# Attention backward: the last value and key gradient sums written in bfloat16 over their float32 tiles, with a third buffer of turned gradients

## The chip, the core and the metric

The kernel runs on one core of one Trainium2 chip. The metric is the device time of one execution in microseconds, the median of several executions. A profile of one execution is given as well; its times are those of that execution.

## What is computed

The reference is a gated mix of an attention block and a state-space convolution, with all gradients. Only the attention's gradients matter here. Cut to them:

```python
qkv = (x @ wqkv).reshape(B, S, 3, H, Dh).transpose(2, 0, 3, 1, 4)   # S 2048, H 32, Dh 18
q, k, v = qkv[0], qkv[1], qkv[2]
p = softmax(einsum("bhqd,bhkd->bhqk", q, k) * Dh ** -0.5)
o = einsum("bhqk,bhkd->bhqd", p, v)
out = g * (o @ wo) + (1 - g) * b          # g: a sigmoid gate, b: the convolution
# and the gradients of out, by jax.vjp, for x, wqkv, wo, the convolution's parameters and the gate
```

For a head the kernel needs dV (the sum over queries of p times dO), dQ and dK (sums over keys and over queries of dS = p * (dP - row sum)). They are stored in one array in DRAM, `dqkv_d`, which a later stage multiplies with the weights and with x.

## The kernel before

**Stages.** Projections and preparations come first (to about 205 us in the profile), then the attention with its backward pass in one long interleaved loop (to about 2197 us), then the convolution with its gradients, and the output products (to the end). The change touches the attention loop alone, which is called the attention stage below.

**Units.** The 32 heads are worked in 8 groups of 4 (`g`), the 2048 queries in 4 blocks of 512 (`b`). A unit is one group and one query block; there are 32. A unit takes 32 steps (`G` counts the steps of all units). A unit's forward part (scores with keys on the partitions, line 723, exponentials at line 799) runs OFF = 39 steps ahead of its backward part (scores again, line 766, exponentials at line 804; dP at line 774; `ds` = dP times p, line 809).

**Order.** The order of the instructions on TensorE (PE), ScalarE (ACT), VectorE (DVE), GpSimd (POOL) and the queue of SyncE (SP) is that in which this loop emits them (`manual_schedule`, line 436). Nothing is moved past anything else on the same engine. Each step has one slot of eight for a part of the sums (lines 677 and 728 to 758): value gradient in slots 0 and 1, query gradient in 2 and 3, a turn of `ds` tiles on PE in 4 and 7, key gradient in 5 and 6. So eight steps handle one key block `kq` of 512 keys, and the four of a unit take `kq` 0 to 3. All sums and turns pass through one PSUM buffer (`accB`, line 588): the next one's first matmul waits until DVE has taken the one before.

**The sums.** For a key block, dV and dK are added up over the four query blocks in float32 tiles in SBUF, four for dV (`dvacc`, line 606) and four for dK (`dkacc`, line 643): a copy at b = 0, an add in place at b = 1 and 2 (lines 612 and 649). At b = 3 the add writes to a bfloat16 tile `gb` instead, which comes from `grad_tile` (line 526) and has two buffers for all callers. dQ is complete after the four key blocks of each unit, and its last write goes to a `gb` tile too (line 630). So a unit with b < 3 takes one `gb` tile and a unit with b = 3 takes nine, in the order v0 k0 v1 k1 v2 k2 v3 q k3, where a k comes five steps after its v, the next v three steps after that, q two steps after v3, and k3 three after q. With two buffers, a write takes the buffer of the write before the last: q that of k2, five steps later, k3 that of v3, five steps later, and the others one that was written eight steps before.

**Storing.** Two steps after a sum is complete `store_grad` (line 529) puts a transposing DMA of the `gb` tile on SP's queue (line 532, to one of two `gT` buffers), and four steps later `pack` copies `gT` without its padding to `dtk` on POOL (line 536) and starts the DMA to `dqkv_d` from POOL's queue (line 537). A `gb` buffer is free when its transposing DMA has landed, a `gT` buffer when POOL has read it.

**SP's queue.** It also starts the 512 transposing DMAs of `ds` (line 817), which the key gradient sums read as `dsT` (line 639), and the loads of the next K, Q, V pieces. A waiting DMA on it holds all behind it. `ds` has five buffers, freed by those DMAs, among others.

The lines that decide the order of the tiles (`nm` V, Q or K, `h` the half of a sum):

```python
SLOTS = {0: ("V", dv_half, 0), 1: ("V", dv_half, 1), 2: ("Q", dq_half, 0), 3: ("Q", dq_half, 1), 5: ("K", dk_half, 0), 6: ("K", dk_half, 1)}
...
if nm == "Q" and kq == NQ - 1:
    at(("pre", G + 2), lambda g=g, b=b: store_grad(UN[(g, b)].pop("dqa"), g, 0, b * TPQ))
elif nm in "KV" and b == NQ - 1:
    at(("pre", G + 2), lambda g=g, kq=kq, nm=nm: store_grad(DKV.pop((nm.lower(), g, kq)), g, 1 + "KV".index(nm), kq * TPQ))
```

Of the kernel before, what the change touches and what calls it, by code (L numbers as in the profile page):

```python
# [11 lines left out]
BF = mybir.dt.bfloat16  # L12
# [5 lines left out]
P = 128  # L18


def build(tc, aps, dbg_aps=None, stages=("s1", "attn", "post", "s4", "final")):
# [7 lines left out]
    def mm(out, lhsT, rhs, start=True, stop=True, **kw):  # L29
        return nc.tensor.matmul(out, lhsT=lhsT, rhs=rhs, start=start, stop=stop, **kw)  # L30
# [13 lines left out]
    HP = 32  # L44
# [17 lines left out]
    with ExitStack() as gctx:  # L62
# [53 lines left out]
        with ExitStack() as ctx:  # L116
            s1 = ctx.enter_context(tc.tile_pool(name="s1", bufs=1))
            work = ctx.enter_context(tc.tile_pool(name="s1work", bufs=2))
# [310 lines left out]
        if "attn" in stages:  # L429
            KB = 512  # L430
            NQ = S // KB
            TPQ = KB // P
            DA = HP
            NFILL = {"V": 1, "Q": 0, "K": 0}
            with ExitStack() as ctx:
# [3 lines left out]
                work = ctx.enter_context(tc.tile_pool(name="awork", bufs=2))  # L439
# [41 lines left out]
                DKV = {}  # L481
# [42 lines left out]
                    return f0, f1, f2  # L524

                def grad_tile():
                    return work.tile([P, KB], BF, tag="gb", bufs=2, name="gb")

                def store_grad(gb, g, which, t0):
                    c0 = which * D + g * 4 * DH  # L530
                    gT = work.tile([P, TPQ, 4, HP], BF, tag="gT", bufs=2, name="gT")
                    nc.sync.dma_start_transpose(out=gT.rearrange("p t a b -> p t (a b)"), in_=gb)

                    def pack():
                        dtk = work.tile([P, TPQ, 4, DH], BF, tag="dtk", bufs=1, name="dtk")
                        nc.gpsimd.tensor_copy(dtk, gT[:, :, :, 0:DH])
                        nc.gpsimd.dma_start(dqkv_d[:, t0:t0 + TPQ, c0:c0 + 4 * DH], dtk.rearrange("p t a b -> p t (a b)"))
                    packs.append((now[0] + 4, pack))
# [10 lines left out]
                def by_pe(p):  # L549

                    return {NPF: 0, NPF + 1: 1}.get(p, 2)
# [15 lines left out]
                def ds_tiles(U, p):  # L567

                    n = by_pe(p)
                    return [U["ds"][2 * p + 2 - n + x][:, 3, :] for x in range(n)], [(n, lambda: U["dsT", p][:, 2 - n:2, 3 * TPQ:, :])]  # L570
# [26 lines left out]
                def dv_half(g, b, kq, h, acc):  # L597
                    U = UN[(g, b)]
                    for ii in (2 * h, 2 * h + 1):
                        for j in range(4):  # L600
                            mm(acc[HP * j:HP * (j + 1), :], lhsT=U["dOa"][:, ii, j, :], rhs=U["eb"].pop((kq, ii, j)),
                               start=(ii == 0), stop=(ii == 3), tile_position=(0, HP * j))

                    def ev():
                        if b == 0:
                            DKV[("v", g, kq)] = work.tile([P, KB], F32, tag="dvacc", bufs=4, name="dvacc")
                            nc.vector.tensor_copy(DKV[("v", g, kq)], acc)
                            return
                        a_ = o_ = DKV[("v", g, kq)]
                        if b == NQ - 1:  # L610
                            o_ = DKV[("v", g, kq)] = grad_tile()
                        nc.vector.tensor_tensor(o_, a_, acc, op=A.add)  # L612
                    return ev

                def dq_half(g, b, kq, h, acc):
                    U = UN[(g, b)]
                    for n_ in (2 * h, 2 * h + 1):
                        for j in range(4):
                            mm(acc[HP * j:HP * (j + 1), :], lhsT=grp_t[g]["Ktok", kq][:, n_, HS * j:HS * j + HP], rhs=U["ds"][TPQ * kq + n_][:, j, :],
                               start=(n_ == 0), stop=(n_ == 3), tile_position=(0, HP * j))  # L620

                    def ev():
                        if kq == 0:
                            U["dqa"] = work.tile([P, KB], F32, tag="dqa", bufs=1, name="dqa")
                            nc.vector.tensor_scalar(U["dqa"], acc, c_scale, None, op0=A.mult)
                            return
                        a_ = o_ = U["dqa"]
                        if kq == NQ - 1:
                            o_ = U["dqa"] = grad_tile()
                        nc.vector.scalar_tensor_tensor(o_, acc, c_scale, a_, op0=A.mult, op1=A.add)  # L630
                    return ev

                def dk_half(g, b, kq, h, acc):
                    U = UN[(g, b)]
                    o_ = acc[:, 2 * h * P:2 * (h + 1) * P]
                    for qb in range(TPQ):
                        for j in range(4):
                            mm(o_[HP * j:HP * (j + 1), :].rearrange("p (a b) -> p a b", b=P), lhsT=grp_t[g]["Qtok", b][:, qb, HP * j:HP * (j + 1)],
                               rhs=U["dsT", 2 * kq + h][:, :, j * TPQ + qb, :], start=(qb == 0), stop=(qb == TPQ - 1), tile_position=(0, HP * j))

                    def ev():
                        if b == 0:
                            DKV[("k", g, kq)] = work.tile([P, KB], F32, tag="dkacc", bufs=4, name="dkacc")
                            nc.vector.tensor_copy(DKV[("k", g, kq)], acc)
                            return
                        a_ = o_ = DKV[("k", g, kq)]
                        if b == NQ - 1:
                            o_ = DKV[("k", g, kq)] = grad_tile()
                        nc.vector.tensor_tensor(o_, a_, acc, op=A.add)
                    return ev  # L650

# [50 lines left out]
                for G in range(NTOT + OFF + 24):  # L702
# [4 lines left out]
                    if G < NTOT:  # L707
                        u, s = divmod(G, NST)
                        g, b = units[u]
# [11 lines left out]
                    if r1:  # L721
                        g, b, i, j0 = r1
# [8 lines left out]
                    if ("f1", G) in todo:  # L731
                        acc = accB("accF")
                        evs.append(todo.pop(("f1", G))[0](acc))
                        e_done[0] += 1.4
                    elif G == NST + 5:
                        evs.append(turn(*do_tile(UN[units[0]])))
                    elif 0 <= m_ < NTOT // 8:
                        u_, kq = divmod(m_, NQ)
                        g, b = units[u_]
                        if slot in SLOTS:  # L740
                            nm, burst, h = SLOTS[slot]
                            if h == 0:
                                acc = accB("acc" + nm)
                                fill(acc, NFILL[nm])
                                burst(g, b, kq, 0, acc)
                            else:
                                evs.append(burst(g, b, kq, 1, acc))
# [4 lines that stand above are left out]
                        else:  # L752
                            p = 2 * kq + (slot == 4)
                            t_, o_ = ds_tiles(UN[(g, b)], p) if by_pe(p) else ([], [])
                            if G % NST == 5 and G // NST - 1 < NU:
                                t2, o2 = do_tile(UN[units[G // NST - 1]])
                                t_, o_ = t2 + t_, o2 + o_
                            evs.append(turn(t_, o_))
                    if r2:
                        g, b, s2 = r2  # L760
# [4 lines left out]
                        kq, ii = s2 // 8, (s2 % 8) // 2  # L765
# [11 lines left out]
                    if G % 8 in (0, 3, 4, 7) and G >= 3:  # L777
                        i_ = (G - 3) // 8 * 4 + {3: 0, 4: 1, 7: 2, 0: 3}[G % 8]
                        u_, i_ = divmod(i_, NT)
                        if 0 <= u_ < NU:  # L780
                            g, b = units[u_]
# [403 lines left out]
        if "final" in stages and "s4" in stages:  # L1185
# [14 lines left out]
            with ExitStack() as ctx:  # L1200
# [128 lines left out]
                work = ctx.enter_context(tc.tile_pool(name="pbwork", bufs=2))  # L1329
# [110 lines left out]
```

## Time and profile before

| | us |
|---|---|
| median of 8 executions | 2980.75 |
| lowest and highest of them | 2970.64, 2983.78 |
| the profiled execution | 2983.78 |
| its span, first to last instruction | 2982.1 |
| busy in it: PE, DVE, ACT, POOL | 2470.2, 2359.3, 2371.6, 1609.3 |
| mean granted TensorE clock | 0.915 |

The span is 1.7 us shorter than the execution's own time. Busy shares are means over stages with different limits, so the profile is read by stage below: the attention stage is 2 of the 3 ms. A list of waits says who sat idle, at which line, until what ended; a timeline has the start, the length, the engine, the line and the operation of each instruction, merged where alike ones follow each other, and in brackets the idle time before it and what ended that. `SPq` is SP's queue; the length of a DMA there is that of its issue, waits for its data included, not of the transfer.

### The profile page before, as it was taken

Reading aid. Unit: us, or ns where it says so; the run is one execution under the profiler, and the core shown is the slowest. Engines: PE = TensorE matmul, PEld = TensorE weight load, DVE = VectorE, ACT = ScalarE, POOL = GpSimd, SP = SyncE. Lnnn points to the kernel's source line nnn. Section 1 sums busy time; section 2 is a strip of 40 time slices with the busy share of each in tenths; the row PEclk is TensorE's granted clock in tenths of the full one; section 3 lists DMA queues with packets and bytes.
Section 4 is the critical chain, followed back from the end, with each engine's and each line's share of the span. In section 5 each row is a group of like instructions: output and inputs, shape, how many; then the busy total and the mean of one; then the engine's idle time right before and its main releaser. Section 6 shows DMA issues by size and latency. Waiting matters only on the chain.

```text
span 2982.1 us, 69573 instructions
## 1 busy us (share of the span) xinstructions
PE 2470.2 (83%) x27132; PEld 1186.3 (40%) x27132; DVE 2359.3 (79%) x4147; ACT 2371.6 (80%) x2765; POOL 1609.3 (54%) x2653
## 2 busy tenths in 40 slices
PE   4768988998998898899899898889847877876779
PEld 2332333332333233233333233323226777776457
DVE  4435998998988899799899899989837888889634
ACT  2449999999999999899999999999636777675111
POOL 1028887888887788778788888787010000000010
PEclk8877999999999999999999999999768888887889
DMA  8755889989989989998988999998688877872886
GB/s 226 159 147 109 157 156 168 162 159 169 170 148 163 169 155 166 163 158 154 174 158 158 167 159 159 164 161 148 121 190 223 205 202 207 211 191 69 244 209 133
DMA packets 1293344, 499.99 MB, mean 168 GB/s; under 512 B 1187775, under 2 KB 1263137, under 8 KB 1283797
## 3 DMA queue, kind: packets, MB, share of 16 engines
q1 hardware_dynamic: 1264500, 434.91, 76.8%
q0 software_dynamic: 20624, 53.26, 7.4%
q10 hardware_dynamic: 7888, 7.38, 0.9%
q8 instruction: 212, 3.47, 0.5%
q14 instruction: 120, 0.98, 0.1%
HBM read 144.48 MB, written 99.69 MB: 82 GB/s over the span
## 4 chain that ended last, share of the span: by engine, by line
ACT 34%; DVE 23%; PE 21%; DMA 8%; issue 7%; POOL 4%; SPq 3%; ACTq 0%; DVEq 0%; POOLq 0%
ACT eb L804 20%; ACT PT L799 13%; PE ps_P L30 7%; DVE ds L809 6%; DVE tz L995 3%; DVE HG L999 2%; DVE tz L998 2%; PE accV L30 2%; PE turn_p L558 2%; PE ps_dx L30 2%; DMA gT<-gb 2%; DVE pq L1065 2%; PE accK L30 1%; PE ps_dwq L30 1%; POOL et L358 1%
## 5 line engine op out<-in xcount | busy, mean ns | idle before, releaser
L809 DVE TENSOR_TENSOR ds<-ps_P,PT 128x512 bf16<-128x512 f32 x2048 | 1312.5, 683 | 124.0 <-PE ps_P L30 83.0
L804 ACT ACTIVATE eb<-ps_P 128x1024 bf16<-128x1024 f32 x1024 | 1095.4, 1070 | 75.8 <-PE ps_P L30 74.9
L799 ACT ACTIVATE PT<-ps_P 128x1024 bf16<-128x1024 f32 x1024 | 1097.9, 1074 | 3.5 <-PE ps_P L30 2.3
L30 PE MATMUL ps_P<-dOaT,VaT_g 32*128 32x512 bf16 x2048 | 583.3, 392 | 31.1 <-DVE ds L809 15.9
L358 POOL TENSOR_TENSOR et<-eG,eT 128x448 f32<-128x448 f32 x576 | 542.7, 963 | 10.7
L30 PE MATMUL ps_P<-QaT_g,KaT_g 32*128 32x512 bf16 x2048 | 413.2, 395 | 144.4 <-ACT PT L799 128.4
L30 PE MATMUL ps_P<-KaT_g,QaT_g 32*128 32x512 bf16 x2048 | 410.0, 393 | 2.2 <-ACT eb L804 1.6
L30 PEld LDWEIGHTS <-KaT_g 32*128 32x128 bf16 x2048 | 147.5, 91 | 480.4 <-issue 465.7
L358 POOL TENSOR_TENSOR Eo<-et,et 128x448 bf16<-128x448 f32 x288 | 327.2, 1136 | 20.8
L1101 POOL TENSOR_TENSOR SS<-m 128x96 f32<-128x96 f32 x18 | 8.1, 448 | 557.8 <-ACT m L1099 557.8
L30 PEld LDWEIGHTS <-QaT_g 32*128 32x128 bf16 x2048 | 115.7, 91 | 289.0 <-issue 267.5
L30 PE MATMUL accO<-PT,Vtok_g 128*32 128x512 bf16 x2048 | 213.4, 404 | 0.0
L30 PE MATMUL accV<-eb,dOa 128*32 128x512 bf16 x2048 | 185.4, 395 | 28.1 <-ACT eb L804 28.1
L30 PE MATMUL accK<-dsT,Qtok_g 128*32 128x256 bf16 x4096 | 167.7, 287 | 4.0 <-DMA dsT<-ds 2.8
L558 PE MATMUL turn_p<-ident_bf,ds 128*128 128x128 bf16 x1664 | 138.1, 227 | 31.4 <-DVE gb L630 30.9
L30 PE MATMUL accQ<-ds,Ktok_g 128*32 128x512 bf16 x2048 | 160.0, 390 | 2.3 <-DVE gb L612 1.9
L957 ACT COPY E1e<-etp 128x1024 bf16<-128x1024 bf16 x144 | 135.9, 1042 | 19.7 <-PE etp L956 14.3
L563 DVE COPY dsT<-turn_p 128x1024 bf16<-128x1024 bf16 (+1 forms) x224 | 144.2, 644 | 4.5 <-PE turn_p L558 4.5
L30 PEld LDWEIGHTS <-Vtok_g 128*32 128x32 bf16 x2048 | 53.5, 93 | 225.7 <-issue 224.9
L30 PEld LDWEIGHTS <-E1n 128*128 128x128 bf16 x2304 | 96.6, 108 | 100.1 <-issue 99.7
L30 PE MATMUL yp<-Rw,E1n 128*128 128x30 bf16 x1152 | 67.8, 232 | 82.6 <-DVE Rw L1020 68.0
L558 PEld LDWEIGHTS <-ds 128*128 128x128 bf16 x1664 | 101.2, 101 | 80.1 <-issue 80.1
(247 smaller groups left out, 3703.8 us busy)
## 6 DMA issues: line engine op xcount, KB each, us to landing
E_d<-Eo POOLq DMA_DIRECT2D x144, 256.0 KB, 3.8
E1n<-E_d SPq DMA_DIRECT2D x36, 1024.0 KB
xs<-xb_d SPq DMA_DIRECT2D x18, 1024.0 KB
T0w<-Kp_d SPq DMA_DIRECT2D x18, 1024.0 KB
Md_d<-mst SPq DMA_DIRECT2D x36, 288.0 KB
dsT<-ds SPq DMA_TRANSPOSE x512
dqkv_d<-dtk POOLq DMA_DIRECT2D x96, 72.0 KB, 4.5
QKV_d<-stg SPq DMA_DIRECT2D x12, 504.0 KB
```

The costliest lines, as they stand in the source:

```text
L30: return nc.tensor.matmul(out, lhsT=lhsT, rhs=rhs, start=start, stop=stop, **kw)
L358: nc.gpsimd.tensor_tensor(out, a, b, op=op)
L558: nc.tensor.transpose(pt_[:, x, qb, :], t_[:, qb * P:(qb + 1) * P], ident_bf)
L563: nc.vector.tensor_copy(o_(), pt_[:, x:x + n])
L799: nc.scalar.activation(U["PT"][i, j // 2], ps, ACT.Exp)
L804: nc.scalar.activation(e, ps, ACT.Exp)
L809: nc.vector.tensor_tensor(U["ds"][i][:, j, :], ps, U["PT"][i, j // 2][:, j % 2, :], op=A.mult)
L957: nc.scalar.copy(E_[:, 4 * q:4 * q + 4], pt_)
L995: nc.vector.tensor_tensor(tz, HG[:, :, k - 1, :].unsqueeze(1).to_broadcast([P, 2, 4, CB]), ZZ, op=A.mult)
L998: nc.vector.tensor_tensor(t0v, t0v, UVk[:, :, :, k, :], op=A.add)
L999: nc.vector.tensor_tensor(HG[:, :, k, :].rearrange("p (r s) c -> p r s c", s=2), t0v, t1v[:, ::-1], op=A.add)
L1065: nc.vector.tensor_tensor(o.rearrange("p a b n c -> p a b (n c)"), a_.rearrange("p b n c -> p b (n c)").unsqueeze(1).to_broadcast([P, 2, 2 ...
```

## The change

The last adds of dV and dK (b = 3) no longer take a `gb` tile. They write their bfloat16 result into the first half of the bytes of the float32 tile that they read, through a view of it as bfloat16, and the transposing DMA reads that view. Only dQ's last write still takes a `gb` tile, and there is one buffer for it instead of two. The turned gradients `gT` have three buffers instead of two; a `gb` and a `gT` buffer are both 1 KB of a partition, so the space is the same.

```diff
                 def grad_tile():
-                    return work.tile([P, KB], BF, tag="gb", bufs=2, name="gb")
+                    return work.tile([P, KB], BF, tag="gb", bufs=1, name="gb")
+
+                def in_place(t_):
+
+                    return t_.bitcast(BF)[:, 0:KB]
...
                 def store_grad(gb, g, which, t0):
                     c0 = which * D + g * 4 * DH
-                    gT = work.tile([P, TPQ, 4, HP], BF, tag="gT", bufs=2, name="gT")
+                    gT = work.tile([P, TPQ, 4, HP], BF, tag="gT", bufs=3, name="gT")
...
                         if b == NQ - 1:
-                            o_ = DKV[("v", g, kq)] = grad_tile()
+                            o_ = DKV[("v", g, kq)] = in_place(a_)
                         nc.vector.tensor_tensor(o_, a_, acc, op=A.add)
...
                         if b == NQ - 1:
-                            o_ = DKV[("k", g, kq)] = grad_tile()
+                            o_ = DKV[("k", g, kq)] = in_place(a_)
                         nc.vector.tensor_tensor(o_, a_, acc, op=A.add)
```

## The prediction

> **What bounds the kernel now.** I read the page first: span, slices, shares of the chain that ended last.
>
> ```profile
> span 2982.1 us, 69573 instructions
> ...
> DVE  4435998998988899799899899989837888889634
> ACT  2449999999999999899999999999636777675111
> ...
> PEclk8877999999999999999999999999768888887889
> DMA  8755889989989989998988999998688877872886
> ...
> ACT 34%; DVE 23%; PE 21%; DMA 8%; issue 7%; POOL 4%; SPq 3%; ACTq 0%; DVEq 0%; POOLq 0%
> ```
>
> In the attention stage (slices 4 to 28) ACT stands at 9 nearly throughout: its exponentials set the pace, with DVE, PE and the DMA engines close behind. Where nothing is late, dQ's last half-sum of one unit and of the next start 58.92 us apart on PE (312.33, 371.25, 430.17), 1.84 us a step. The list of waits says what ACT's gaps come from:
>
> ```profile
> ACT eb L804 <- PE ps_P L30: 74.9, 68, 7.6
> ...
> DVE gb L630 <- DMA gT<-gb: 34.1, 7, 8.0
> ...
> PE turn_p L558 <- DVE gb L630: 30.9, 8, 7.4
> ```
>
> (total us, times, longest). DVE waits 7 times before dQ's last write for the transposing DMA that still holds its `gb` buffer; PE then waits for DVE's release of the PSUM buffer, ACT for PE. All seven are at the end of a group (groups 0 to 6). The first, in the timeline:
>
> ```profile
> 486.47 0.69 DVE L612 TENSOR_TENSOR gb<-dvacc,accV 128x512 bf16<-128x512 f32 x1 [0.18 <-PE accV L30]
> ...
> 489.36 1.22 SPq L532 DMA_TRANSPOSE gT<-gb  x1
> ...
> 490.67 4.20 SPq L817 DMA_TRANSPOSE dsT<-ds  x2
> ...
> 494.08 0.69 DVE L630 SCALAR_TENSOR_TENSOR gb<-accQ,dqa 128x512 bf16<-128x512 f32 x1 [4.33 <-DMA gT<-gb]
> ...
> 494.82 1.01 PE L558 MATMUL turn_p<-ident_bf,ds 128*128 128x128 bf16 x8 [3.76 <-DVE gb L630]
> ...
> 496.41 1.03 ACT L804 ACTIVATE eb<-ps_P 128x1024 bf16<-128x1024 f32 x1 [3.96 <-PE ps_P L30]
> ```
>
> k2's transposing DMA is issued at 489.36 and its landing lets DVE go at 494.08. After the gap PE is slow for a while, which costs more than the gap (here 1.3 us more of ACT by 505):
>
> ```profile
> 490.00:495.00 5.00, 0.88 (x9) 0.39 (x9) 0.92 (x2) 2.45 (x3) 4.55 (x6) 0.75 1.07 162
> 495.00:500.00 5.00, 5.00 (x52) 1.88 (x54) 4.09 (x7) 3.29 (x4) 4.08 (x13) 0.50 0.94 192
> ```
>
> (busy PE, PEld, DVE, ACT, POOL; then the granted clock, 0.50 here; DMA share; GB/s.)
>
> **What the Trainium skill says.** "TensorE: Matmul & The Clock Gate", Part 1, has the clock halve after an idle window of about 3.4 us and return after a busy one. The trace agrees on the halving, but in group 6 a PE gap of 2.27 us was enough, so short gaps may cost too. "DMA: Bandwidth & Descriptors", Anatomy of one DMA, says that the issuing sequencer, not the DMA engine, waits for semaphores. That agrees: k2's sum was written at 481.6, yet its DMA stood behind other issues until 489.36. "VectorE: DVE Perf Modes", Mode 2×_2P, warns of overlapping operands where one source is read by both ports, and says that tensor_tensor can't run so. The adds here have two sources; no run shows the in-place narrowing yet.
>
> **The change part by part.**
>
> The adds: 32 of dV, 32 of dK, in number as before. Writing bfloat16 they take 689 and 688 ns (median), writing float32 in place 689 and 687. I take 0; two-sided bound for the new overlap: 64 x ±10 ns, under 1 us.
>
> Waits removed: the instruction lists of both kernels have the same order on all five engines; only waits differ. The last adds of dV and dK and dQ's last write at b = 3 now wait for PE alone. What each stall cost is the distance between dQ's last half-sum in that unit and in the next, less 58.92: 5.63, 5.36, 6.08, 8.53, 4.37, 6.21, 4.95, sum 41.1 us (34.1 of DVE's wait, the rest slow PE). Group 7 ends with no unit after it; its write waits for PE (2.00), not for a DMA: 0.
>
> Waits added: (1) a `dvacc` or `dkacc` buffer is now free for the next group only when its DMA has landed. The tightest is k3's: lands at 509.0, rewritten near 560. Cover 50 us, cost 0; behind it on DVE would stand `ds`, and so ACT. (2) dQ's single `gb` waits for the DMA of a unit before, 58.92 us earlier: 0. (3) The `ds` write after dQ's takes over a wait for an older `dsT` DMA, landed at 481.4, used at 490.5: 0.
>
> The third `gT`: before, SP waits for POOL to read a `gT` (4 lines of 13.3, 7.7, 4.4 and 2.6 us, 28.0 in all, at most 2.1 each), with `dsT` transposes queued behind. Most goes. The gT issues just ahead of the stalls took 1.22 us, the unwaited length, so on the path I take 0 (bound: 0 to 3 us gain). POOL's packs are not hurried by it: their chain at the stage's end (a `dtk` copy and its DMA, about 3.6 us each, starting 2186.3) stays.
>
> What is late next: the last key half-sum of the unit, 5.35 us after dQ's in every undisturbed unit. It reads `dsT`, whose last transposing DMA SP issues right behind k2's and which DVE's stall did not hold up. From the records of issue and completion:
>
> ```
> group                      0      1      2      3      4      5      6
> dQ's last half-sum    489.36 731.83 976.89 1218.64 1463.11 1703.15 1945.31
> that dsT lands        495.27 738.78 983.55 1228.03 1467.90 1711.05 1949.87
> minus start + 5.35      0.6    1.6    1.3    4.0   -0.6    2.6   -0.8
> ```
>
> Without DVE's stall, PE would wait there 10.1 us in all. To that I add 3 us for a slow PE after the longer ones (group 6's 2.27 us gap cost 4.95, so up to 2.7 each for three: bounds 0 to 8), and 2 us for half-sums in the unit that follows: there, the DMA for the first key block's second half-sum comes 9 issues (13.3 us) after that one, whose issue ended 3.9 us after dQ's half-sum in group 0, and lands 2.3 later: at 19.5, against a need at 5.35 + 8 x 1.84 = 20.1 plus what was lost by then. That is about 1 us of margin with landings that vary by 2 (bounds 0 to 8).
>
> Sum: 41.1 - 10.1 - 3 - 2 = 26 us gained. The profiled execution (2983.78, span 2982.1 plus 1.7 around it) would take 2957.8; it was the slowest of eight, 3 us over the median, so from the median: 2980.75 - 26 = **2954.8, say 2955 us**.
>
> **The rivals.**
>
> Full return (15%): DMA latencies fall because the slow stretch no longer bunches POOL's stores, and `dsT` is in time. For: in group 3 the landing was late by a zero-fill DMA on POOL's queue (7 us), an accident of timing. Against: DMA share over 1.0 around each stall, moved closer together. 2980.75 - 41 = 2940.
>
> The `dsT` wait takes most (23%): each of the five waits cools PE as group 6 shows (8 us) and the next units' margins are used up (8). For: half-sums with no margin stand in the profile already (at 721 and 905, ACT losing 1.2 and 1.7). 41 - 10 - 16 = 15, and with latencies 1 us worse 41 - 10 - 16 - 5 = 10: 2966 to 2971.
>
> Nothing to measure (7%): `dsT` takes all of it, or the view is held by a wait that the lists don't show. Within 6 us of 2981.
>
> Slower (5%): the schedule comes to the SP queue 6 us earlier in each group while its issue rate stays, and the half-sums of the last key block and of the next unit's wait in turn, each with a slow PE after it. It decides once the added waits exceed 41.1 / 7 = 5.9 us a group; with landings like the one of 7 us in group 3 everywhere (5 us later than now), that is 1.4 + 5 + 0.7 = 7.1 a group: 2989.
>
> **How the numbers follow.** A difference of 0.2% (6 us) is what a measurement of this kernel can tell from none. Likeliest 50%: 2955, itself between 2948 and 2962. Faster: 0.50 + 0.15 + 0.23 = 0.88; same 0.07; slower 0.05. The range runs from the full return, 2940, to the bulk of the second rival, 2970: outside are the last two cases and the tails.
>
> **What would show it.** Right: DVE's wait before line 630 for `gT<-gb` gone from the list; PE or PEld waiting for `dsT<-ds` about 10 us more, at the last key half-sum of groups 1, 2, 3 and 5; ACT's wait for PE at line 804 down from 74.9 to some 50; the add rows still at 0.69 us; the convolution stage unchanged in length. Wrong: no `dsT` waits (full return), or long ones with clocks of 0.50 behind them in every group (second rival, or slower).

## The result, and the profile after

| | before | after |
|---|---|---|
| median, executions | 2980.4 us, 32 | 2967.4 us, 12 |
| lowest and highest | 2970.6, 2989.4 | 2958.0, 2973.2 |
| profiled execution, its span | 2983.8, 2982.1 | 2961.6, 2959.9 |
| mean granted TensorE clock in it | 0.915 | 0.918 |

The ratio is 0.9953, 95% interval 0.9942 to 0.9964: 13 us faster where 26 were predicted (2955; the range was 2940 to 2970). The two profiled executions lie 22 us apart, since before's was slower than its median and after's faster; the medians decide on the size. Before's 32 executions include the eight of the table further up.

The page first: span, slices, and the shares of the chain that ended last.

```profile
span 2959.9 us, 69509 instructions
...
DVE  4436998998999899899899889989927888889634
ACT  2449999999999999999999999999636777674111
...
PEclk8877999999999999999999999999857888887889
DMA  8865899989989999988988998998788877872885
...
ACT 36%; DVE 24%; PE 23%; DMA 7%; issue 6%; SPq 2%; POOL 0%; ACTq 0%; DVEq 0%; POOLq 0%
```

The slices hardly differ, as was to be expected: the gain is 0.5%, spread over seven places. The list of waits says more (total us, times, longest).

```profile
ACT eb L808 <- PE ps_P L30: 57.1, 63, 5.8
...
DVE dkacc L653 <- PE accK L30: 29.6, 66, 6.1
...
PE accK L30 <- DMA dsT<-ds: 19.8, 9, 5.5
```

DVE's 34.1 us for `gT<-gb` are gone from the list, and with them PE's 30.9 for DVE. New is PE, waiting for `dsT<-ds` at the key half-sums (2.8 us before), and DVE behind it. ACT lost 74.9 us to PE and still loses 57.1. At the adds, the list of lines by form shows no cost of the narrowing in place: the same 688 and 687 ns (after the bar: total us, mean ns of one; then the idle time before them and what ended it).

```profile
L616 DVE TENSOR_TENSOR dvacc<-dvacc,accV 128x512 f32<-128x512 f32 x64 | 44.0, 688 | 11.7 <-PE accV L30 11.7
...
L616 DVE TENSOR_TENSOR dvacc<-dvacc,accV 128x512 bf16<-128x512 f32 x32 | 22.0, 688 | 5.9 <-PE accV L30 5.6
...
L653 DVE TENSOR_TENSOR dkacc<-dkacc,accK 128x512 bf16<-128x512 f32 x32 | 22.0, 687 | 22.6 <-PE accK L30 21.9
```

One group end in the timeline, that of group 5:

```profile
1686.49 1.25 SPq L536 DMA_TRANSPOSE gT<-dkacc  x1
...
1687.81 0.69 DVE L634 SCALAR_TENSOR_TENSOR gb<-accQ,dqa 128x512 bf16<-128x512 f32 x1 [0.29 <-PE accQ L30]
1687.84 7.14 SPq L821 DMA_TRANSPOSE dsT<-ds  x2
...
1696.40 1.05 PE L30 MATMUL accK<-dsT,Qtok_g 128*32 128x256 bf16 x16 [3.84 <-DMA dsT<-ds]
...
1697.49 0.69 DVE L653 TENSOR_TENSOR dkacc<-dkacc,accK 128x512 bf16<-128x512 f32 x1 [4.49 <-PE accK L30]
...
1698.02 1.02 ACT L808 ACTIVATE eb<-ps_P 128x1024 bf16<-128x1024 f32 x1 [4.13 <-PE ps_P L30]
```

dQ's last write goes through at once. But k2's transposing DMA still stands on SP's queue ahead of the last one of `ds` of this unit (the first of the two from 1687.84 on; the second is the next unit's), so the last half-sum waits 3.84 us, ACT waits 4.13, and the group end loses 4.72 us where it lost 6.21. Behind such a wait PE's clock is down (busy PE, PEld, DVE, ACT, POOL; granted clock; DMA share; GB/s), here at the ends of groups 0 and 5:

```profile
505.00:510.00 5.00, 3.24 (x40) 1.46 (x40) 2.99 (x5) 3.60 (x5) 3.97 (x9) 0.84 1.15 176
510.00:515.00 5.00, 4.86 (x33) 1.01 (x30) 3.21 (x5) 3.97 (x5) 4.76 (x6) 0.50 0.79 152
...
1692.00:1697.00 5.00, 1.16 (x19) 0.69 (x18) 1.00 (x2) 1.89 (x3) 4.31 (x6) 0.93 1.04 164
1697.00:1702.00 5.00, 4.88 (x48) 1.68 (x38) 3.82 (x6) 3.70 (x4) 2.70 (x9) 0.73 1.00 184
```

**Where the time came from.** I take the prediction's measure: the distance between dQ's last half-sums of two units in turn, less 58.92 us. A second profiled execution of the changed kernel is the run `after_again` below.

```
loss at the end of group    0     1     2     3     4     5     6     sum   other units
before                    5.63  5.36  6.08  8.53  4.37  6.21  4.95   41.1       6.0
predicted                                                            15.1
after                     4.01  4.07  2.78  7.76  2.22  4.72  2.66   28.2       3.7
after, again              1.41  6.74  5.54  5.66  0.15  4.43  6.95   30.9       2.7
```

("Other units" are the distances inside groups 0 to 6.) The group ends give back 12.9 us in the first profile, 10.2 in the second, and the medians differ by 13. How the loss falls varies: the profile of run 1 below, whose group ends are the same but for one `gT` buffer, has 21.7 us at the ends and 9.9 in other units. The two together are steadier: 47.1 us before, and 31.9, 33.6 and 31.6 in these three profiles. The other 9.3 of the 22.2 us between the two profiles lie elsewhere (first half-sum 3.9 us earlier, 2.3 in other units, 2.5 in the last two units, 0.7 in the tail), and other profiles scatter there by as much.

### The profile page after: what moved, and what is told of

Its sections match the earlier page's. It is cut to its first block, busy times and chain, and to the rows that moved or that the text cites. A ratio compares the mean times of both kernels' runs of the same rounds, so it can differ in the third digit from the quotient of the medians.

```text
span 2959.9 us, 69509 instructions
## 1 busy us (share of the span) xinstructions
PE 2468.5 (83%) x27132; PEld 1188.1 (40%) x27132; DVE 2360.3 (80%) x4147; ACT 2371.9 (80%) x2765; POOL 1608.5 (54%) x2653
## 4 chain that ended last, share of the span: by engine, by line
ACT 36%; DVE 24%; PE 23%; DMA 7%; issue 6%; SPq 2%; POOL 0%; ACTq 0%; DVEq 0%; POOLq 0%
ACT eb L808 21%; ACT PT L803 13%; DVE ds L813 7%; PE ps_P L30 7%; DVE tz L999 3%; DVE HG L1003 2%; DVE tz L1002 2%; PE accV L30 2%; DMA dsT<-ds 2%; PE ps_dx L30 2%; PE turn_p L562 2%; PE accK L30 2%; DVE pq L1069 2%; PE ps_dwq L30 1%; PE accO L30 1%
## 5 line engine op out<-in xcount | busy, mean ns | idle before, releaser
L808 ACT ACTIVATE eb<-ps_P 128x1024 bf16<-128x1024 f32 x1024 | 1095.1, 1070 | 58.3 <-PE ps_P L30 57.1
L30 PE MATMUL ps_P<-dOaT,VaT_g 32*128 32x512 bf16 x2048 | 581.9, 390 | 31.6 <-DVE ds L813 16.9
L30 PE MATMUL accK<-dsT,Qtok_g 128*32 128x256 bf16 x4096 | 164.3, 282 | 21.0 <-DMA dsT<-ds 19.8
L961 ACT COPY E1e<-etp 128x1024 bf16<-128x1024 bf16 x144 | 135.8, 1040 | 19.8 <-PE etp L960 14.6
L30 PEld LDWEIGHTS <-Qtok_g 128*32 128x32 bf16 x4096 | 88.6, 97 | 86.9 <-issue 65.4
```

Of the source, the lines that this page charges most:

```text
L808: nc.scalar.activation(e, ps, ACT.Exp)
L961: nc.scalar.copy(E_[:, 4 * q:4 * q + 4], pt_)
```

## The experiments

The theory (A): the one wait of dQ's last write for k2's transposing DMA was all that the change could remove, and what remains at the group ends is late `dsT`, because the transposing DMAs of dV and dK stand on SP's queue among those of `ds`. Rivals: the third `gT` buffer had a part in it; other buffers' waits had; the load on the DMA engines, the clock, or a store on POOL's queue is what remains. The ratios are to the kernel before on the same chip, whose median was 2973.9 us for runs 1, 3, 4 and 5, 2977.6 for 2, 6 and 7, and 2976.5 and 2974.6 for the two pairs of 8.

**1. In place, but two `gT` buffers.**

```diff
-gT = work.tile([P, TPQ, 4, HP], BF, tag="gT", bufs=3, name="gT")
+gT = work.tile([P, TPQ, 4, HP], BF, tag="gT", bufs=2, name="gT")
```

> The change without its third buffer of turned gradients: in-place last sums, one buffer for dQ's result, two buffers for gT. Theory A (the whole gain is the removed wait of dQ's last write for the transposing DMA of k2; the third buffer frees SP only where nothing waits): as the changed kernel, 2967 us, within 4. Theory B (the third buffer carries a part, because SP stands behind POOL's copies with the ds transposes queued behind): 2973 us or more, and the losses at the ends of the groups grow from 28 us towards 35.

Measured 2959.4 us, ratio 0.9956 (0.9939 to 0.9972), against 0.9953 with three, and the losses at the group ends did not grow towards 35 (21.7 us). The third buffer does nothing that can be measured.

**2. Half of the change: only dK's last sums in place, dV's in `gb` (two buffers), two `gT` buffers.**

Against the kernel before, the edit is this (cut):

```diff
-o_ = DKV[("k", g, kq)] = grad_tile()
+o_ = DKV[("k", g, kq)] = in_place(a_)
```

> Half of the change alone: only dK's last sums are written in place; dV's still take one of the two gb buffers, and there are two gT. With it dQ's last write takes the buffer of v2, written ten steps earlier, instead of k2's, five steps earlier. Theory A (all of the gain is that one wait, q's for k2's transposing DMA): DVE's waits for gT<-gb before dQ's last write are gone or below 2 us in all, the losses at the seven group ends sum to 20 to 28 us as in the changed kernel, ratio 0.9953 within 0.002. Theory B (the other sums' buffers were part of the gain, through waits that the lists put down to something else): half the gain or less, ratio 0.9975 or higher.

Measured 2963.9 us, ratio 0.9960 (0.9945 to 0.9976). The waits for `gT<-gb` on DVE are gone; the key half-sum waits stand in the list instead, as in the changed kernel:

```profile
ACT eb L808 <- PE ps_P L30: 63.1, 67, 5.1
...
PE accK L30 <- DMA dsT<-ds: 23.3, 11, 4.8
```

The group ends lose 31.4 us, above the 20 to 28 expected and about what the changed kernel's second profile has (30.9). As far as these ratios can tell, freeing the one buffer that dQ's last write takes is the whole effect: A stands.

**3. The five DMAs later.** At the ends of groups 0 to 6, the transposing DMAs of k1, v2, k2, v3 and k3 are issued 20 steps later, in the next unit. Their packs and stores on POOL follow them; nothing else moves.

```diff
+late = 20 if g + 1 < NG and 2 * kq + "VK".index(nm) >= 3 else 0
-at(("pre", G + 2), lambda ...: store_grad(...))
+at(("pre", G + 2 + late), lambda ...: store_grad(...))
```

> The changed kernel, but in groups 0 to 6 the last five of the eight transposing DMAs of value and key gradients (k1, v2, k2, v3, k3) are put on SP's queue 20 steps (37 us) later, which the in-place tiles allow since they are not written again for 32 steps. Theory A (what is left at the ends of the groups, 28 us, is the last key half-sums waiting for ds transposes that come late behind these DMAs on SP's queue and on the DMA engines): the losses fall below 12 us and the time to 2945 to 2955. Theory B (the ds transposes are late there for the loads of the next group's pieces and POOL's stores, and the gradient transposes matter little): 2963 to 2968. Theory C (the loss is no DMA matter, but PE's clock or the shared PSUM buffer): no change, 2967.

Measured 2942.7 us, ratio 0.9893 (0.9872 to 0.9914): faster than both kernels, with intervals that don't touch. The losses at the group ends: 3.99, 0.32, 0.72, 4.31, 0, 0, 0, in sum 9.3 us. At the end of group 5 the unit's last `dsT` DMA (the first of the two at 1682.49) is now issued 2.47 us ahead of dQ's last half-sum, where it was 0.70 us behind it. It lands at 1689.64, 0.67 us before the last key half-sum reads it (the second of the two below). Neither that nor ACT waits; in the windows ACT is busy throughout and the clock is 1.00.

```profile
1682.49 5.05 SPq L822 DMA_TRANSPOSE dsT<-ds  x2
...
1688.42 0.62 PE L30 MATMUL accK<-dsT,Qtok_g 128*32 128x256 bf16 x16
...
1690.31 0.62 PE L30 MATMUL accK<-dsT,Qtok_g 128*32 128x256 bf16 x16
```

```profile
1682.00:1687.00 5.00, 4.54 (x53) 1.45 (x50) 4.54 (x8) 5.00 (x7) 4.83 (x6) 1.00 0.86 158
1687.00:1692.00 5.00, 4.66 (x62) 1.76 (x59) 4.61 (x8) 5.00 (x7) 4.38 (x10) 1.00 1.42 162
```

What changed is when the last `dsT` DMA is through SP's queue. In us after dQ's last half-sum; in the earliest case, the units with b = 1, its issue ends at -2.2, it lands at 0.0, and it is needed at 5.35:

```
group                   0     1     2     3     4     5     6
after   issue ends    3.39  4.37  3.98  3.69  2.13  4.75  1.82
        lands         5.11  7.90  7.66 10.85  4.32  9.22  4.78
delayed issue ends   -0.67  2.65  0.10  0.79  0.27  1.02 -0.25
        lands         1.22  5.95  1.92  7.43  2.53  4.68  2.80
```

Its issue ends 4 to 7 us late, part of which is a longer issue (in group 5 it takes 4.05 us instead of 1.44), and the transfer adds up to 5 more (group 3, 7.2 us from the end of the issue to the landing instead of 2.2). Moving the DMAs takes 1.7 to 4.1 us off the first. What group 0 still loses, 3.99 us, is no late `dsT`: its last half-sum starts on time, and the loss comes 50 us later, where the delayed packs run (waits from 525 to 552: total us, times, longest).

```profile
POOL dtk L540 <- DMA dqkv_d<-dtk: 5.6, 1, 5.6
...
DVE dOa L522 <- POOL prod L516: 1.9, 1, 1.9
...
PE turn_p L562 <- DVE dkacc L648: 1.6, 1, 1.6
```

A pack waits for the store of the pack before it, and a product that DVE needs (`prod`) stands behind it on POOL. So the delay is not free everywhere.

**4. No transposing DMA of dV and dK at all.** This kernel leaves the turning of the 64 value and key gradient tiles out; POOL stores other data in their place.

```diff
+if which == 0:
     gT = work.tile(...)
     nc.sync.dma_start_transpose(...)
+else:
+    gT = dOa2[0]
```

> The changed kernel with the 64 transposing DMAs of value and key gradients left out: POOL packs a tile of other data in their place and stores that, so the value and key parts of the gradients are not the reference's. It bounds what these DMAs cost in all. Theory A (they make the ds transposes late): losses at the ends of the groups from 28 us to under 6, time 2938 to 2948. Theory B (the next group's loads do): losses above 15 us, time above 2955.

Measured 2927.6 us, ratio 0.9845 (0.9827 to 0.9863), and the group ends lose 0.8 us in all. POOL's stores are issued as before, so what remains there comes from these DMAs (and from POOL's waits for them), not from the stores. They cost 0.0108, some 32 us, of which about 7 lie in the tail (788.9 us from the last unit's half-sum to the end, 795.8 in the changed kernel), the chain of packs at the stage's end.

**5. Each of the 64 issued twice, to the same `gT`.**

```diff
+if which:
+    nc.sync.dma_start_transpose(out=gT.rearrange(...), in_=gb)
```

> The changed kernel with each of the 64 transposing DMAs of value and key gradients issued twice in a row to the same tile: the suspected load doubled, no other wait added. Theory A (SP's queue and the DMA engines are full at the ends of the groups): each second copy takes SP 1.2 to 1.5 us and lands about as much later, eight in a group, of which margins absorb half: 30 to 60 us more, 2997 to 3027, slower than the kernel before. Theory B (there is room on the queue and the lateness comes from single collisions): under 10 us more.

Measured 3165.7 us, ratio 1.0648 (1.0625 to 1.067), far above what either theory expected. The experiment did more than double a load:

```profile
453.87 1.23 SPq L536 DMA_TRANSPOSE gT<-dkacc  x1
...
458.72 1.19 SPq L538 DMA_TRANSPOSE gT<-dkacc  x1
...
459.96 4.86 SPq L823 DMA_TRANSPOSE dsT<-ds  x2
```

The second writes the tile that the first writes, so SP stands from 455.10 until the first has landed (458.71), and everything on its queue with it. SP's list of waits has 152 us of this (90.7 for dK, 61.3 for dV), and the kernel is 0.0695 or some 207 us above the changed one. The next run takes that wait away.

**6. Each of the 64 issued twice, the second to a spare tile.**

```diff
-gT = work.tile([P, TPQ, 4, HP], BF, tag="gT", bufs=3, name="gT")
+gT = work.tile([P, TPQ, 4, HP], BF, tag="gT", bufs=2, name="gT")
...
+if which:
+    gS = work.tile([P, TPQ, 4, HP], BF, tag="gS", bufs=1, name="gS")
+    nc.sync.dma_start_transpose(out=gS.rearrange(...), in_=gb)
```

> The changed kernel with two gT buffers, in which each of the 64 transposing DMAs of dV and dK is followed by a second one of the same source to a spare tile that nobody reads (results unchanged). The spare tile is written again three steps later at the earliest, so the second copy seldom waits, unlike the one that went to the same gT. Theory A (what remains at group ends is the load of these DMAs on SP's queue and the DMA engines; leaving them out saved 0.0108, some 32 us): as much again or somewhat more, 32 to 60 us, ratio 1.006 to 1.016, the dsT waits at the group ends 2 to 4 us longer each and also in the middle of b = 3 units. Theory B (only the wait for the first copy's landing made the earlier doubling slow, and a DMA more costs SP nothing that anyone waits for): within 0.3% of the changed kernel, 0.993 to 0.998.

Measured 3027.6 us, ratio 1.0177 (1.0156 to 1.0197): 0.0224 or 67 us above the changed kernel, a little more than A's 32 to 60, and nothing like B. The waits are where A has them:

```profile
ACT eb L811 <- PE ps_P L30: 114.1, 91, 8.1
...
PE accK L30 <- DMA dsT<-ds: 68.5, 23, 7.5
...
PEld L30 <- DMA dsT<-ds: 44.4, 21, 7.8
```

The group ends lose 51.0 us and the other units 40.5, nearly all in the units with b = 3. With the 152 us of run 5's waits, these 67 come near its 207. So such a DMA costs about 0.5 us when it is taken away (32 / 64) and 1.0 when another is added (67 / 64), as one would expect of a queue with less and less slack.

**7. One store on POOL's queue moved.** In the changed kernel's profile a zero fill of `xb_d` is issued at 1205.75, a microsecond ahead of the slow `dsT` at the end of group 3. It is put 40 steps later, in the changed kernel and in the delayed one.

```diff
-at(("pre", 216 + 56 * r), lambda r=r: put_zero(r))
+at(("pre", 216 + 56 * r + (40 if r == 6 else 0)), lambda r=r: put_zero(r))
```

> The changed kernel with one zero-fill store on POOL's queue, the one that fell into the end of group 3, put 40 steps later; all else as changed. Theory A (the 7.4 us transfer of dsT at the end of group 3 is a collision with that store, and the accident costs what group 3 loses over its neighbours): group 3's loss falls from 7.8 to 3 or 4 us, the dsT wait of 5.5 us there to about 2, the other six ends as they were; time 4 us less than the changed kernel, ratio to the kernel before about 0.994. Theory B (the landing is late from the group end's own DMAs, and the store has nothing to do with it): group 3's loss stays at 7 to 8 us, ratio 0.9953 as the changed kernel.

> Both edits together: in groups 0 to 6 the transposing DMAs of the last five value and key sums 20 steps later, and the one zero-fill store 40 steps later. Theory A: the delayed version's remaining loss of 4.3 us at group 3's end goes, the rest stays as in the delayed version; ratio 0.988, about 3 us less than the delayed version (0.9893). Theory B (the zero fill is not the cause): 0.989 again, group 3 still at 4 us.

Measured 2960.9 us, ratio 0.9946 (0.9929 to 0.9963), and 2942.9 us, 0.9886 (0.9864 to 0.9908). Group 3's loss falls from 7.76 to 3.15 us and from 4.31 to 0. The two lines of the changed kernel, then the same two of the one with the store moved (in each, the first of the two DMAs is the unit's last):

```profile
1206.81 7.40 SPq L821 DMA_TRANSPOSE dsT<-ds  x2
...
1216.43 1.05 PE L30 MATMUL accK<-dsT,Qtok_g 128*32 128x256 bf16 x16 [5.47 <-DMA dsT<-ds]
```

```profile
1213.37 3.92 SPq L821 DMA_TRANSPOSE dsT<-ds  x2
...
1219.08 1.04 PE L30 MATMUL accK<-dsT,Qtok_g 128*32 128x256 bf16 x16 [1.58 <-DMA dsT<-ds]
```

In the other profiles with the store in place and the gradients' DMAs neither delayed nor doubled nor left out, group 3 loses 4.5 to 7.4 us. Both profiles with the store moved lie below their like, and in them that `dsT` lands 3.3 and 2.0 us after the end of its issue instead of 7.2 and 6.6: the collision is likely real, with one profile of each kernel. But 3 us are too few for the ratios to show, and other units took them back in these profiles (8.0 and 13.6 us outside the group ends).

**8. PE kept busy during the wait.** Twelve spare matmuls (overwritten by the sum that follows) ahead of the seven half-sums that wait in the changed kernel's profile; and, as a control, at the same places two units later (the last of them one unit later), where nothing waits.

```diff
+if nm == "K" and (4 * g + b, kq) in ((4, 0), (7, 3), (11, 3), (15, 3), (20, 0), (23, 3), (28, 0)):
+    fill(acc, 12, 2)
 evs.append(burst(g, b, kq, 1, acc))
```

> The changed kernel with 12 spare matmuls of 256 columns (some 1.3 to 2 us, overwritten by the sum that follows) put on PE just ahead of seven second key half-sums: the last one of the unit in groups 1, 2, 3 and 5, and that of the first key block of the next group's first unit at the ends of groups 0, 4 and 6. These are the half-sums that wait for dsT in the changed kernel's profile, so the spare work falls into the wait. Theory A (of the 28 us that the seven group ends still lose, 19.6 are these waits and the rest, 8.6, is PE at a halved clock after them): the clock no longer falls to 0.50 behind the waits of about 2 us (it still does in group 3, 5.5 us), the losses at group ends fall by 5 to 8 us to about 21, ratio 0.9925 to 0.994. Theory B (the rest is not the clock, but a backlog that PE works off anyway at 90% busy): the losses stay at 26 to 30 us, ratio 0.995 to 0.997.

> The control: the same 12 spare matmuls at the same two places of a unit, but seven times in units two later, where no half-sum waits. Theory A (PE has about 0.5 us to spare in 5 us, so 1.3 to 2 us of work too many delays the exponentials by part of that, and nothing is gained): 3 to 8 us slower than the changed kernel, ratio 0.9965 to 0.998. Theory B (dips of this size are hidden behind the exponentials that are already fed): within 1 us of it, ratio 0.9953.

The first: 2962.5 us, ratio 0.9958 (0.9944 to 0.9973). The control: 2968.7 us, 0.9976 (0.9964 to 0.9988), so seven such fills cost up to 0.0023, some 7 us, where nobody waits (1.1 us each in its profile). At the waits, the clock does what A says: at the end of group 0 the clock stays at 1.00 where it was 0.84 and 0.50,

```profile
508.00:513.00 5.00, 4.60 (x54) 2.45 (x52) 3.10 (x7) 3.68 (x5) 4.87 (x9) 1.00 1.10 150
513.00:518.00 5.00, 4.68 (x47) 1.27 (x45) 4.41 (x8) 5.00 (x6) 4.47 (x6) 1.00 1.01 213
```

and the group ends lose 18.7 us instead of 28.2. The time is nevertheless the changed kernel's, as B has it: in this profile other units lose 14.7 us instead of 3.7. Two more runs ask whether that is chance.

> The changed kernel once more, to see how the losses fall in a second profiled execution: in the first one the seven group ends lost 28.2 us and all other units 3.7 us. Theory A (where a unit loses beyond the group ends is chance, the landings of dsT vary by 2 us and several half-sums have no margin): ends again 24 to 32 us, the others anything from 3 to 12 us, in other units than the first time. Theory B (the pattern is fixed by the schedule): ends 27 to 29 us, others 3 to 5 us, in units 7 and 27 again. The ratio as before, 0.9953 within 0.0015.

> The changed kernel with the 12 spare matmuls ahead of seven half-sums, once more: its first profile had 18.7 us at the group ends but 14.7 us in other units (3.7 without the spare matmuls), so that its time was that of the changed kernel. Theory A (those 14.7 us are chance, as in the other profiles, where 4 to 14 us are lost there): ends again 16 to 22 us, others 4 to 10 us. Theory B (a group end that is left earlier makes the units that follow later): others 12 to 18 us again, in the units before the group ends, 7, 11, 15 and 19. The ratio within 0.0015 of 0.9958 in both.

The changed kernel again: 2962.4 us, ratio 0.9955 (0.9939 to 0.9971); group ends 30.9 us, others 2.7. With the fills again: 2964.7 us, 0.9961 (0.9939 to 0.9983); group ends 13.9, others 5.9. What a given group end loses varies by up to 4.3 us between the two profiles of the changed kernel. The lower sum at the group ends repeats (18.7 and 13.9, against 21.7 to 30.9 in the two profiles of the changed kernel, in run 1 and in the control), and the lower time doesn't. Whether the large losses elsewhere were chance stays open: in the first profile with fills, ends and other units together lose 33.4 us, as much as without them, which is what B says; in the second they lose 19.8, but that execution took 2948.9 us, the lowest of its eight and 16 below their median, so its profile doesn't stand for it. What takes the gain back in the median is not settled.

## Why the prediction was half right

**The wait removed, 41.1 us: right.** DVE's wait for `gT<-gb` is gone in every group, and by run 2 this one wait is the whole effect, within what the ratios can tell.

**What is late next: the right place, mis-sized.** The prediction left 15.1 us at the group ends; 28.2 remained. The terms, in the order of the sum, with PE's wait for `dsT<-ds` read in the window of each group end:

```
                                              predicted   after
last key half-sum (groups 1, 2, 3, 5)           10.1       14.3   (2.5 + 2.5 + 5.5 + 3.8)
half-sums of the unit that follows (0, 4, 6)       2        5.3   (1.8 + 1.3 + 2.2)
the rest: PE at a lower clock, and its backlog     3        8.6   (28.2 - 14.3 - 5.3)
```

The table of landings took the records of before as they stood. Without the stall, in groups 1, 2, 3 and 5 `dsT` lands about 1 us later after dQ's half-sum than before (7.90, 7.66, 10.85, 9.22 against 6.95, 6.66, 9.39, 7.89). The 2 us for the following unit was the step that failed most in proportion: the margin "about 1 us, with landings that vary by 2" was worked out for group 0, called a small cost, and was used up at three ends of seven. The 3 us for the clock counted only the longer waits; in group 0 one of 1.76 us was followed by a window at 0.50. The second profile splits differently (16.2 us of waits, 14.7 of the rest), and run 1's has 21.7 us at the ends in all, so each term of the last column is one execution's. What holds in all three profiles is that ends and other units together lose 32 to 34 us, where the forecast (15.1, and the 6.0 of before) had 21.

**Nothing for the third `gT`, the adds and the added waits: right.** Run 1 for the first, the add rows at 688 and 687 ns for the second, and no wait of DVE for a DMA at `dvacc`, `dkacc` or `gb` in the list for the third. One statement with it was wrong: SP's waits for POOL at the `gT` tiles (28 us in four lines before) did not mostly go. They are 23.1 in four lines after, with three buffers; by run 1 they cost nothing that can be measured.

**The rivals.** Full return (2940) failed: the DMA latencies did not fall (from the end of the issue to the landing, the median of the 512 DMAs of `ds` is 2.6 us in both profiles). The second rival, "the `dsT` wait takes most", had the number, 2966 to 2971, with 2967 measured, by the two terms that the forecast undersized, and its "latencies 1 us worse" is about what the landings show; I should have weighed it above the forecast, since before's own profile showed half-sums without margin. Its picture of a collapse in every group was too strong, since in the second profile group 4's end loses 0.15 us and group 0's 1.41. Slower and nothing are out.

## What to carry to other kernels

A wait that is removed on one engine is worth its length less what the next late event keeps, and that event must be priced with the queue as it will be then: landings taken from the profile with the stall in it were about 1 us too early here. Where work that nobody waits for soon shares an in-order queue with work on the path, moving it to a time when the queue has room can bring more than another buffer: here that took the ratio from 0.9953 to 0.9893, more than the change itself. To price a load by doubling it, see that no wait comes with the second copy. And where losses come from late DMAs, one profile doesn't say where they fall: here one group end lost 0.15 us in one execution and 2.22 in another of the same kernel.

## What the runs showed of the hardware

- PE's clock fell to 0.50 behind waits of about 2 us (1.76 us at 507.42 in group 0, then 0.50 in the window from 510 to 515), and once behind one of 0.29 us at 716.45: from 712 to 716.6 PE was busy 3.87 of 4.6 us, and the clock was 0.50 in the window from 716.6 to 720. The Trainium skill, "TensorE: Matmul & The Clock Gate", Part 1, names an idle window of about 3.4 us; here shorter waits were enough, with other short gaps before them. A dozen spare matmuls in the wait of group 0 held the clock at 1.00.
- A second DMA to a tile whose first has not landed holds the whole of SP's queue: 3.6 us between two issues at 455 and 459. The Trainium skill, "DMA: Bandwidth & Descriptors", Anatomy of one DMA, has the issuing sequencer do such waiting, and the trace agrees.
- A unit's last transposing DMA of `ds` took 2.2 us from the end of its issue to its landing in the units with b = 1, and 7.2 with a zero-fill store issued a microsecond ahead of it; with that store moved, it took 3.3 at the same place.
- VectorE writes the bfloat16 sum over its own float32 operand at 688 ns for 128x512, as into another tile.
